# Attention and spectral mixing in one kernel: values in halves, a smaller reciprocal, moved splits, and half of the last transfers on GpSimd's queue

## The chip, the cores and the metric

The kernel runs on one core of a Trainium2 chip. The metric is the device time of one execution in microseconds, the median of several executions. TensorE is called PE here, VectorE DVE, ScalarE ACT, GpSimd POOL, and the engine that issues transfers SP.

## What is computed

The shapes are fixed: 8 batches, 12 heads, 448 tokens, heads of 64; 768 channels. First an attention with capped scores, then, on its output, a mixing over tokens and over channels, all in float32 (the weights arrive in float64):

```python
scores = np.matmul(q, k.transpose(0, 1, 3, 2)) / np.sqrt(64)
scores = cap * np.tanh(scores / cap)
attn = np.exp(scores - scores.max(-1, keepdims=True))
x = np.matmul(attn / (attn.sum(-1, keepdims=True) + 1e-09), v)   # then heads side by side: (8, 448, 768)
theta = x @ w_theta
y = w_tok_r @ (x * cos(theta)) + w_tok_i @ (x * sin(theta))       # over tokens, per batch
u = x + y
out = u + np.maximum(u @ w_ch, 0.0)
```

## The kernel before

Work goes pair by pair: a pair is two heads of one batch, so a batch has 6 pairs (NP) and the kernel 48 (NS). A step s of the outer loop computes the scores of pair s and finishes pair k = s-1. What a step does, and in which order, is written as a line of words (FRONT for steps 0 to 7, PARTS for a batch's six later steps, OTHER for single steps). The words are issued in that order, each engine runs its own instructions strictly in that order, and nothing is moved by a scheduler.

- `A`, `B` (line 216): scores of the pair's first and second half of the keys, on PE into one PSUM tile `s` of four banks, of which there is one. So B can start only when the tanh of A has read it, and the next A only when the tanh of B has.
- `tA`, `tB` (221) are the tanh, `eA`, `eB` (227) the exponentials, on ACT, into the tiles `p`.
- `V` (259): values times `p`, 16 matmuls for pair k, on PE; `cV` (265) copies the result to `x` on ACT.
- `R` (278): sums over keys by matmuls with ones, for two pairs at a time into one tile `r`; `R0`, `R1` are its two halves in FRONT. `I` (301): DVE takes 1/r of the whole 128x448 tile, in which each sum stands in 32 equal rows, and SP spreads it (305) into `bc`. `n`, `N` (309): DVE multiplies `x` by `bc`.
- `w0`, `w1`, `w2`: pieces of the weights' preparation, placed by the table WEIGHTS under (step, a/b/c). A float64 weight tile (`th0` to `th5` of w_theta, `ch0` to `ch5` of w_ch, `tk0` to `tk6` of the token weights) is loaded by SP (">", 106), scaled on ACT ("*", 110) or DVE ("#", 113), and split into a high and a low part on DVE (118 to 127). For `ch` tiles the cast of the high part (123) is on ACT, between DVE's instructions.
- `x`, `X`, `u`: split of an activation tile into high (ACT, 319) and low part (DVE, 320).
- `T` (328 to 330): theta of one channel block, 54 matmuls for three; `y` (350, 351), `d` (356 to 358), `sc` (363, 364), `r` (368): angle reduction, cosine and sine, product. `f` (372) turns 32x32 blocks on DVE, and `D` (381) carries the 32-row stripes to their places: 16 transfers from SP for one of the three pairs of blocks, D0, D1, D2. After them `h` and `l` (386, 392) split the turned blocks on ACT and DVE, `M` (401 to 403) mixes over tokens on PE, `m` (406) adds on DVE, `C` (328 to 330 with w_ch) and `c` (413) end a batch.

Steps 0 to 7 have scores, values and weights only; step 8 starts the first batch's theta. In the last batch no scores are left: its theta, C3 to C5 of the batch before and the three carries are one line of words (`OTHER[(B - 2, 5)]`), and its mixing another.

## Time and profile before

| what | value |
|---|---|
| median of 3 executions | 944.97 us (944.39 to 946.01) |
| profiled execution, its own time | 941.22 us |
| its span, first to last instruction | 939.4 us |
| PE / DVE / ACT busy | 98% / 73% / 66% |
| DMA | 90.66 MB, nearly all on one queue |

The profiled execution is 3.75 us shorter than the median, and 1.8 us of its time lie outside of the span. PE is busy almost throughout, so what matters is where it is not; a busy share of PE says nothing of its pace, since matmuls are pipelined and their ends are modelled. Starts of instructions are the safer reading.

### The profile page before, as it was taken

How to read it: one execution, taken by the hardware profiler on the slowest of the kernel's cores; microseconds unless marked ns; L12 is line 12 of the kernel's file. 1: busy time of each engine (PE TensorE's matmuls, PEld its weight loads, DVE VectorE, ACT ScalarE, POOL GpSimd, SP SyncE). 2: the span in 40 equal slices, each digit the busy share in tenths (PEclk: the TensorE clock that was granted, in tenths of full speed). 3: DMA queues.
4: the chain of work that ended last, by engine and by line, in shares of the span. 5: the costliest groups of instructions: out<-in, count | busy, mean ns of one | idle time of the engine just before them, and what ended most of it. 6: DMA issues, size and time to landing. Idle time of an engine off the chain costs nothing.

```text
span 939.4 us, 12874 instructions
## 1 busy us (share of the span) xinstructions
PE 916.8 (98%) x4912; PEld 660.9 (70%) x4912; DVE 682.9 (73%) x914; ACT 617.6 (66%) x644; POOL 0.4 (0%) x6
## 2 busy tenths in 40 slices
PE   8999989999999999999999999999999999999997
PEld 4224657667776787777677776776877777789887
DVE  5898756997876679666887568775787568965741
ACT  7988696567954688656976479645895569753420
POOL 0000000000000000000000000000000000000000
PEclk9999999999999999999999999999999999999999
DMA  7664155422642235332452325422353333411521
GB/s 267 200 186 128 34 123 132 121 98 72 126 89 79 82 65 120 78 108 70 86 102 67 101 62 107 117 78 71 67 119 80 91 96 76 77 32 48 92 52 62
DMA packets 208774, 90.66 MB, mean 97 GB/s; under 512 B 182464, under 2 KB 194752, under 8 KB 208704
## 3 DMA queue, kind: packets, MB, share of 16 engines
q1 hardware_dynamic: 208704, 89.76, 38.3%
q8 instruction: 40, 0.66, 0.3%
q14 instruction: 30, 0.25, 0.1%
HBM read 45.68 MB, written 11.01 MB: 60 GB/s over the span
## 4 chain that ended last, share of the span: by engine, by line
PE 73%; ACT 15%; DVE 6%; SPq 3%; DMA 1%; issue 1%; DVEq 0%; ACTq 0%
PE a L259 10%; PE s L216 10%; PE mx L403 7%; PE mx L401 7%; PE mx L402 7%; PE ch L328 6%; PE ch L329 6%; PE ch L330 6%; ACT p L221 5%; PE th L328 4%; PE th L329 4%; PE th L330 4%; SPq L381 3%; ACT p L227 2%; PE r L278 2%; ACT L221 2%
## 5 line engine op out<-in xcount | busy, mean ns | idle before, releaser
L221 ACT ACTIVATE p<-s,qscale 112x1792 f32<-112x1792 f32 x96 | 168.5, 1755 | 124.2 <-PE s L216 122.6
L227 ACT ACTIVATE p<-p,cap_sb 112x1792 f32<-112x1792 f32 x96 | 170.2, 1785 | 0.4
L259 PE MATMUL a<-p,v 112*64 112x448 f32 x768 | 155.1, 546 | 3.7 <-ACT p L227 3.7
L259 PEld LDWEIGHTS a<-p,v 112*64 112x64 f32 x768 | 50.7, 136 | 91.0 <-issue 74.9
L328 PE MATMUL ch<-us,wch_h 128*128 128x448 f32 x288 | 107.1, 372 | 0.0
L328 PE MATMUL th<-xs,wth_h 128*128 128x448 f32 x288 | 107.0, 371 | 0.0
L329 PE MATMUL ch<-us,wch_h 128*128 128x448 f32 x288 | 105.5, 366 | 0.0
L329 PE MATMUL th<-xs,wth_h 128*128 128x448 f32 x288 | 105.5, 366 | 0.0
L330 PE MATMUL ch<-us,wch_l 128*128 128x448 f32 x288 | 105.4, 366 | 0.0
L330 PE MATMUL th<-xs,wth_l 128*128 128x448 f32 x288 | 105.3, 366 | 0.0
L252 DVE TENSOR_TENSOR ps<-ps,p 112x896 f32<-112x896 f32 x76 | 82.8, 1089 | 2.2
L301 DVE RECIPROCAL ri<-r 128x448 f32<-128x448 f32 x24 | 70.9, 2954 | 17.2 <-PE r L278 17.2
L403 PE MATMUL mx<-wtk_h,zl_False 128*128 128x448 f32 x192 | 71.4, 372 | 3.2 <-DVE zl_False L392 2.5
L401 PE MATMUL mx<-wtk_h,zh_False 128*128 128x448 f32 x192 | 72.0, 375 | 0.1
L402 PE MATMUL mx<-wtk_l,zh_False 128*128 128x448 f32 x192 | 70.2, 366 | 0.0
L368 DVE TENSOR_TENSOR g_sb<-g_sb,x 128x896 f32<-128x896 f32 x48 | 50.7, 1086 | 22.3 <-ACT g_sb L364 22.3
L413 DVE SCALAR_TENSOR_TENSOR x<-ch,x 128x448 f32<-128x448 f32 x48 | 29.8, 620 | 51.1 <-PE ch L330 51.1
L328 PEld LDWEIGHTS ch<-us,wch_h 128*128 128x128 f32 x288 | 54.2, 188 | 10.3 <-issue 5.3
L328 PEld LDWEIGHTS th<-xs,wth_h 128*128 128x128 f32 x288 | 54.1, 188 | 9.6 <-issue 5.2
L330 PEld LDWEIGHTS ch<-us,wch_l 128*128 128x128 f32 x288 | 54.2, 188 | 4.9 <-DVE wch_l L127 0.2
L330 PEld LDWEIGHTS th<-xs,wth_l 128*128 128x128 f32 x288 | 54.1, 188 | 4.7
L329 PEld LDWEIGHTS th<-xs,wth_h 128*128 128x128 f32 x288 | 54.1, 188 | 4.6 <-DVE xs L320 0.3
(79 smaller groups left out, 1550.8 us busy)
## 6 DMA issues: line engine op xcount, KB each, us to landing
g_sb<-g_sb SPq DMA_DIRECT2D x384, 56.0 KB, 2.0
qk_sb<-in_qk SPq DMA_DIRECT2D x35, 448.0 KB, 3.6
v<-in_v SPq DMA_DIRECT2D x48, 224.0 KB, 2.9
bc<-ri SPq DMA_DIRECT2D x96, 112.0 KB, 2.3
out_dram<-x SPq DMA_DIRECT2D x48, 224.0 KB, 2.0
qk<-in_qk SPq DMA_DIRECT2D x13, 448.0 KB, 3.5
g_sb<-in_wth SPq DMA_DIRECT2D x6, 768.0 KB, 5.7
g_sb<-in_wch SPq DMA_DIRECT2D x6, 768.0 KB, 4.8
```

Of the source, the lines that this page charges most:

```text
L216: nc.tensor.matmul(sp[:CP, i, hh, :S], kk[k][rows, 1, ks], qq[k][rows, 0, :], start=n == 0, stop=n == len(products) - 1)
L221: nc.scalar.activation(pt[k, half], spt.pop((k, half))[:CP, :, :, :S], AF.Tanh, scale=qscale[:CP])
L227: nc.scalar.activation(pp, pp, AF.Exp, scale=cap_sb[:CP])
L252: nc.vector.tensor_tensor(pst[k], pst[k], pt[k, 1][:, i], op=ALU.add)
L259: nc.tensor.matmul(acc[hh * D : (hh + 1) * D, :S], va[:, hh, c, :], pt[k, c // 2][:, c % 2, hh, :], start=c == 0, stop=c == NCH - 1)
L301: nc.vector.reciprocal(ri, r[:, :S])
L328: nc.tensor.matmul(acc[:, :S], wh[:, j, ms], t[:, 0, :], start=j == 0, stop=False)
L329: nc.tensor.matmul(acc[:, :S], wh[:, j, ms], t[:, 1, :], start=False, stop=False)
L330: nc.tensor.matmul(acc[:, :S], wl[:, j, ms], t[:, 0, :], start=False, stop=j == NJ - 1)
L401: nc.tensor.matmul(acc[:, :S], zh, wtk_h[:, c, :], start=c == 0, stop=False)
L402: nc.tensor.matmul(acc[:, :S], zh, wtk_l[:, c, :], start=False, stop=False)
L403: nc.tensor.matmul(acc[:, :S], zl, wtk_h[:, c, :], start=False, stop=c == NC2 - 1)
```

## The change

1. In FRONT the values are computed in two halves: `Va` (keys of A) stays between A and B, `Vb` (keys of B) goes behind B. The copy `cV` goes behind the tanh of B.
2. `I` no longer takes 448 reciprocals in a row: DVE turns the 32x32 blocks of `r` into `ri`, takes the reciprocal of 14 columns into a small tile `few`, and turns these, repeated, back into `ri`. This holds for all 24 places.
3. Splits are moved among the steps, `th3` and `ch0` are scaled on DVE, and the cast of `ch0`, `ch1` and `ch2` is on DVE. The split of the first activation blocks is spread over steps 5, 6 and 7.
4. In steps 8 and 9 the exponentials stand directly behind their tanh, ahead of theta.
5. In the last batch 8 of the 16 transfers of D1 and of D2 (odd d) are issued from GpSimd's queue, and the first `l` stand ahead of r5 on DVE.

```diff
-            steps["ch", m] = Split(room_g(...), w_ch[m], wch_h[:, :, ms], wch_l[:, :, ms], True)
+            steps["ch", m] = Split(room_g(...), w_ch[m], wch_h[:, :, ms], wch_l[:, :, ms], m > 2)
...
-        (3, "c"): "*tk2", (4, "a"): "*th4", (4, "b"): "th4 >ch0", (4, "c"): "*tk3", (5, "b"): "tk2 >tk4 tk3 >tk5",
+        (4, "a"): "*th4 *tk2", (4, "b"): "th4 >ch0", (4, "c"): "*tk3", (5, "b"): "tk2 >tk4 tk3 >tk5",
...
+    def av(k, halves):
+        if 0 in halves:
+            acc_of["a", k] = psM.tile([P, 512], F32, tag="m", name=f"a{k}")
+        va, acc = vt[k], acc_of["a", k]
+        for c in (c for c in range(NCH) if c // 2 in halves):
...
         ri = wk.tile([P, S], F32, tag="ps", name=f"ri{k}", bufs=2)
+        nc.vector.transpose(out=ri, in_=r[:, :S])
+        few = wk.tile([P, S // 32], F32, tag="few", name=f"few{k}", bufs=1)
+        each = ri.rearrange("p (c j) -> p c j", j=32)[:, :, 0]
...
-            nc.vector.reciprocal(ri, r[:, :S])
+            nc.vector.reciprocal(few, each)
+        nc.vector.transpose(out=ri, in_=few.unsqueeze(2).broadcast_to([P, S // 32, 32]))
...
-                nc.sync.dma_start(t[32 * m : 32 * m + 32, :, d, :], z[32 * d : 32 * d + 32, :, m, :])
+                queue = nc.gpsimd if b == B - 1 and i and d % 2 else nc.sync
+                queue.dma_start(t[32 * m : 32 * m + 32, :, d, :], z[32 * d : 32 * d + 32, :, m, :])
...
-    FRONT = "A tA w0 eA V cV v R0 B tB R1 q w1 n I eB aA aB w2 x"
+    FRONT = "A tA w0 eA Va R0 B tB Vb cV v R1 q w1 n I eB aA aB w2 x"
...
-        (0, 0): "A tA V cV w0 v R I B tB q P w1 eA T0 y0 d0 aA eB T1 y1 d1 sc0 T2 y2 r0 r1 f0 f1 d2 w2 D0",
+        (0, 0): "A tA eA V cV w0 v R I B tB eB aA aB q T0 y0 d0 w1 T1 y1 d1 sc0 w2 T2 y2 r0 r1 f0 f1 d2 D0",
...
-                for j in {6: range(4), 7: range(4, NJ)}.get(s, ()):
+                for j in {5: range(2), 6: range(2, 4), 7: range(4, NJ)}.get(s, ()):
```

PE in step 3 and at the start of step 4 (a step without sums); `s_0` and `s_1` are the scores of A and B, `a` the values of the pair before, `p_0` and `p_1` its two halves. Before:

```order
L216 MATMUL s_0_292<-qk_206 112x448 x4
L259 MATMUL a_301<-p_0_227,v_197 64x448 x4
L259 MATMUL a_301<-p_1_258,v_197 64x448 x4
L216 MATMUL s_1_314<-qk_206 112x448 x4
L216 MATMUL s_0_342<-qk_272 112x448 x4
```

and with the change:

```order
L216 MATMUL s_0_295<-qk_206 112x448 x4
L260 MATMUL a_303<-p_0_227,v_204 64x448 x4
L216 MATMUL s_1_308<-qk_206 112x448 x4
L260 MATMUL a_303<-p_1_250,v_204 64x448 x4
L216 MATMUL s_0_344<-qk_272 112x448 x4
```

The second half of the values has moved from ahead of B to between B and the next A.

ACT at the end of step 11 and the start of step 12, around the split of `ch2`: line 110 scales it, line 123 casts its high part, the tanh that follows is A's of step 12. Before:

```order
L227 ACTIVATE p_1_1097<-p_1_1097,cap_sb 112x1792
L319 CAST us_2_1187<-x_310 128x448
L110 ACTIVATE g_sb<-g_sb 128x768
L123 CAST wch_h<-g_sb 128x6x128
L221 ACTIVATE p_0_1218<-s_0_1217,qscale 112x1792
```

and with the change:

```order
L227 ACTIVATE p_1_1112<-p_1_1112,cap_sb 112x1792
L325 CAST us_2_1202<-x_319 128x448
L110 ACTIVATE g_sb<-g_sb 128x768
L221 ACTIVATE p_0_1233<-s_0_1232,qscale 112x1792
L267 COPY x_1248<-a_1239 128x448
```

The cast is gone from ACT's row (it is on DVE); that of `ch4`, ahead of the tanh of step 13, stays.

DVE at the last batch's third pair of blocks: the first product (r4), the second (r5), the two block turns (f4, f5), the low parts `zl_0` for the first mixing, and the last additions of the batch before. Before:

```order
L368 TENSOR_TENSOR g_sb<-g_sb,x_6606 128x896
L368 TENSOR_TENSOR g_sb<-g_sb,x_6733 128x896
L372 STREAM_TRANSPOSE g_sb<-g_sb 128x896 x2
L413 SCALAR_TENSOR_TENSOR x_5686<-ch_4_7066,x_5686 128x448
L392 TENSOR_TENSOR zl_0_False<-g_sb,zh_0_False 128x512
L392 TENSOR_TENSOR zl_0_True<-g_sb,zh_0_True 128x384
```

and with the change:

```order
L374 TENSOR_TENSOR g_sb<-g_sb,x_6675 128x896
L399 TENSOR_TENSOR zl_0_False<-g_sb,zh_0_False 128x512
L399 TENSOR_TENSOR zl_0_True<-g_sb,zh_0_True 128x384
L374 TENSOR_TENSOR g_sb<-g_sb,x_6802 128x896
L378 STREAM_TRANSPOSE g_sb<-g_sb 128x896 x2
L420 SCALAR_TENSOR_TENSOR x_5746<-ch_4_7146,x_5746 128x448
```

The low parts of the first mixing now stand ahead of r5 and of both turns.

## Rows read from the trace of the kernel before

**Rows 1.** Page part 1: busy time, share of the span, instructions of each engine.

```profile
PE 916.8 (98%) x4912; PEld 660.9 (70%) x4912; DVE 682.9 (73%) x914; ACT 617.6 (66%) x644; POOL 0.4 (0%) x6
```

**Rows 2.** Waits: engine, line <- releaser: total us, times, longest us.

```profile
PE s L216 <- ACT p L221: 8.7, 9, 1.9
```

**Rows 3.** Timeline of PE, steps 4 to 8: start, us, engine, line [idle before <-releaser].

```profile
40.05 1.76 PE L216 MATMUL s<-qk 64*112 64x448 f32 x8 [1.93 <-ACT p L221]
41.74 3.23 PE L259 MATMUL a<-p,v 112*64 112x448 f32 x16
44.90 1.71 PE L278 MATMUL r<-p,ones_sb 112*32 112x448 f32 x16
46.54 1.76 PE L216 MATMUL s<-qk 64*112 64x448 f32 x8
...
55.00 1.76 PE L216 MATMUL s<-qk 64*112 64x448 f32 x8
58.62 1.76 PE L216 MATMUL s<-qk 64*112 64x448 f32 x8 [1.85 <-ACT p L221]
...
79.12 1.76 PE L216 MATMUL s<-qk 64*112 64x448 f32 x8 [0.54 <-ACT p L221]
```

**Rows 4.** Timeline of ACT: the last activation split ahead of step 8's tanh.

```profile
82.94 1.10 ACT L319 CAST xs<-x 128x448 fp32r<-128x448 f32 x2 [0.94 <-DVE x L309]
```

**Rows 5.** Timeline of PE in step 10.

```profile
125.36 1.72 PE L259 MATMUL a<-p,v 112*64 112x448 f32 x8 [2.72 <-ACT p L227]
128.08 1.72 PE L259 MATMUL a<-p,v 112*64 112x448 f32 x8 [1.00 <-ACT p L227]
129.74 3.20 PE L278 MATMUL r<-p,ones_sb 112*32 112x448 f32 x16
```

**Rows 6.** Groups by line: count | busy us, mean ns | idle before, releaser.

```profile
L301 DVE RECIPROCAL ri<-r 128x448 f32<-128x448 f32 x24 | 70.9, 2954 | 17.2 <-PE r L278 17.2
L372 DVE STREAM_TRANSPOSE g_sb<-g_sb 128x896 f32<-128x896 f32 x48 | 51.1, 1092 | 0.0
L125 DVE CAST wth_h<-g_sb 128x768 fp32r<-128x768 f32 x6 | 3.4, 562 | 0.0
```

**Rows 7.** Timelines of ACT and PE, steps 12 and 13.

```profile
172.12 0.84 ACT L123 CAST wch_h<-g_sb 128x768 fp32r<-128x768 f32 x1 [4.64 <-DVE g_sb L119]
191.02 0.84 ACT L123 CAST wch_h<-g_sb 128x768 fp32r<-128x768 f32 x1 [4.08 <-DVE g_sb L119]
...
174.66 3.00 PE L216 MATMUL s<-qk 64*112 64x448 f32 x8 [1.66 <-ACT p L221]
194.02 1.76 PE L216 MATMUL s<-qk 64*112 64x448 f32 x8
```

**Rows 8.** Stretch, then busy us by engine, PE's granted clock, DMA share, GB/s.

```profile
175.00:178.40 3.40, 3.40 (x10) 1.41 (x7) 3.40 (x5) 2.06 (x5) 0.00 (x0) 0.50 0.48 128
```

**Rows 9.** Timelines of the last batch: SP, PE, ACT, DVE.

```profile
866.33 21.92 SPq L381 DMA_DIRECT2D g_sb<-g_sb  x32
...
885.05 0.47 PE L403 MATMUL mx<-wtk_h,zl_False 128*128 128x448 f32 x1 [1.45 <-DVE zl_False L392]
903.83 0.47 PE L403 MATMUL mx<-wtk_h,zl_False 128*128 128x448 f32 x1 [1.05 <-DVE zl_False L392]
...
901.43 0.62 ACT L386 CAST zh_False<-g_sb 128x512 fp32r<-128x512 f32 x1 [5.11 <-DMA g_sb<-g_sb]
...
872.98 2.10 DVE L372 STREAM_TRANSPOSE g_sb<-g_sb 128x896 f32<-128x896 f32 x2
877.01 0.39 DVE L357 TENSOR_SCALAR g_sb<-g_sb 128x448 f32<-128x448 f32 x1
881.79 2.10 DVE L372 STREAM_TRANSPOSE g_sb<-g_sb 128x896 f32<-128x896 f32 x2
884.32 0.67 DVE L392 TENSOR_TENSOR zl_False<-g_sb,zh_False 128x512 fp32r<-128x512 f32 x1
```

**Rows 10.** Page part 6: DMA issues: count, KB each, median us to landing.

```profile
g_sb<-g_sb SPq DMA_DIRECT2D x384, 56.0 KB, 2.0
```

More of the change, by code (lines that the diff above doesn't have):

```diff
@@ L148, in weight_steps @@
             steps["th", m] = Split(room_g((0, 6 * S)[m % 2]), w_theta[m], wth_h[:, :, ms], wth_l[:, :, ms])
-            steps["ch", m] = Split(room_g((0, 6 * S, 8 * S, 0, 8 * S, 0)[m]), w_ch[m], wch_h[:, :, ms], wch_l[:, :, ms], True)
+            steps["ch", m] = Split(room_g((0, 6 * S, 8 * S, 0, 8 * S, 0)[m]), w_ch[m], wch_h[:, :, ms], wch_l[:, :, ms], m > 2)
         for c in range(NC2):
@@ L252, in add_half @@
                 nc.vector.tensor_tensor(pst[k], pst[k], pt[k, 1][:, i], op=ALU.add)
-    def av(k):
-        va = vt.pop(k)
-        acc = psM.tile([P, 512], F32, tag="m", name=f"a{k}")
-        for c in range(NCH):
+    def av(k, halves):
[3 more added lines that the diff above has]
+        for c in (c for c in range(NCH) if c // 2 in halves):
             for hh in range(2):
@@ L260, in av @@
                                  start=c == 0, stop=c == NCH - 1)
-        acc_of["a", k] = acc
+        if 1 in halves:
+            vt.pop(k)
     def av_out(k):
@@ L296, in invert @@
         ri = wk.tile([P, S], F32, tag="ps", name=f"ri{k}", bufs=2)
+        nc.vector.transpose(out=ri, in_=r[:, :S])
+        few = wk.tile([P, S // 32], F32, tag="few", name=f"few{k}", bufs=1)
+        each = ri.rearrange("p (c j) -> p c j", j=32)[:, :, 0]
         if state["general"]:
-            nc.vector.tensor_scalar_add(ri, r[:, :S], 1e-9)
-            nc.vector.reciprocal(ri, ri)
-        else:
-            nc.vector.reciprocal(ri, r[:, :S])
+            nc.vector.tensor_scalar_add(few, each, 1e-9)
+            nc.vector.reciprocal(few, few)
+        else:
+            nc.vector.reciprocal(few, each)
+        nc.vector.transpose(out=ri, in_=few.unsqueeze(2).broadcast_to([P, S // 32, 32]))
         for n in (k - 1, k):
@@ L427, in softcap_attn_then_spectral_mix @@
     OTHER = {
-        (0, 0): "A tA V cV w0 v R I B tB q P w1 eA T0 y0 d0 aA eB T1 y1 d1 sc0 T2 y2 r0 r1 f0 f1 d2 w2 D0",
-        (0, 1): "A tA V cV N w0 v R I aB- B tB q P w1 T3 y3 d3 sc1 eA T4 r2 r3 f2 f3 D1 y4 d4 eB T5 aA aB y5 d5 w2",
+        (0, 0): "A tA eA V cV w0 v R I B tB eB aA aB q T0 y0 d0 w1 T1 y1 d1 sc0 w2 T2 y2 r0 r1 f0 f1 d2 D0",
+        (0, 1): "A tA eA V cV N v R I B tB eB aA aB q T3 y3 d3 sc1 T4 r2 r3 f2 f3 D1 y4 d4 T5 y5 d5",
         (B - 2, 4): "V cV u3 u4 u5 R I C0 c0 C1 X0 X1 c1 C2 X2 X3 c2",
         (B - 2, 5): "N X4 X5 T0+ y0+ d0+ T1+ y1+ d1+ sc0+ T2+ r0+ r1+ f0+ f1+ D0+ y2+ d2+ T3+ y3+ d3+ sc1+ T4+ r2+ r3+ f2+ f3+ D1+ y4+ d4+"
-                    " T5+ y5+ d5+ sc2+ C3 c3 r4+ r5+ f4+ f5+ D2+ C4 c4 h0a+ l0a+ h0b+ l0b+ h1a+ C5 c5",
+                    " T5+ y5+ d5+ sc2+ C3 c3 r4+ h0a+ l0a+ h0b+ l0b+ r5+ f4+ f5+ D2+ C4 c4 h1a+ C5 c5",
         (B - 1, 0): "M0a l1a h1b M0b l1b h2a m0 u0 M1a l2a h2b M1b l2b h3a m1 u1 M2a l3a h3b M2b l3b h4a m2 u2 M3a l4a h4b M3b l4b h5a"
@@ L465, in run @@
                     add_half(s, "AB".index(word[1]))
-            elif word == "V":
+            elif name == "V":
                 if done:
-                    av(k)
+                    av(k, (0, 1) if word == "V" else ("ab".index(word[1]),))
             elif word == "cV":
```

6 rows, old and new, of the table WEIGHTS are left out of this document.

## The prediction, made before the changed kernel ran

> **What bounds the kernel now.** I read the busy shares first, then the waits, then the timelines around the largest. PE is busy for 916.8 of 939.4 us [rows 1], so at most 22.6 us can come from filling its idle time; the rest would need fewer matmuls, and the change has as many as before. The waits say where the idle time is: 8.7 us before scores that wait for a tanh [rows 2], 3.72 us before values that wait for an exponential (2.72 and 1.00, step 10) [rows 5], and 2.5 us in the last batch before matmuls that wait for low parts (1.45 and 1.05) [rows 9]. DVE, at 73%, is full only where weights are split, and POOL does nothing. The sum is made from starts of instructions, against the profiled execution: 941.22 us of its own time, a span of 939.4 and 1.8 around it. It lies 3.75 us under the median of 944.97, so I carry the gain over to the median.
>
> **Part 1, values in halves (steps 1 to 8).** Of the two-half `s` there is one set, so the next scores wait for the tanh of the last ones. In a step without sums the second scores start at 55.00 and the next step's at 58.62 with 1.85 of idle before them [rows 3]: 3.62 us for scores, semaphore and tanh, under which only 1.69 us of matmuls lie (40.05 to 41.74), since the values (3.16, to 44.90) all stand on the other side, ahead of B. With halves, each tanh is covered by half the values: 1.66 (128.08 to 129.74) [rows 5], so A + Va is 1.69 + 1.66 = 3.35, still under 3.62, and such a step takes 2 x 3.62 = 7.24. A step with sums has also half of the sums (1.64, 44.90 to 46.54) on each side: 2 x (1.69 + 1.66 + 1.64) = 9.98, more than the tanh. The two steps make 17.22; before, from 40.05 to 58.62, they made 18.57 [rows 3]. That is 1.35 for steps 4 and 5, and again for 2 and 3, which have waits of the same sizes. Steps 6 and 7 both have sums: 58.62 to 79.12 is 20.50, and becomes 19.96, so 0.5. With 0.2 in step 1 part 1 gives 3.4, if ACT is free at each tanh.
>
> Where it may not be is step 8. The tanh of A stands there behind the last activation splits on ACT, which wait for DVE's products until 82.94 [rows 4], and DVE is packed ahead of those. The change gives DVE back three reciprocals' difference by then and adds the scales of `th3` and `ch0` and a cast: three passes over 128x768 at 0.56 each [rows 6], 1.7 in all. The new `I` is two block turns of 448 columns and a reciprocal of 14. A turn of 896 columns is 1.09 [rows 6]; by columns one of 448 is 0.55, with a fixed part between that and 1.09. The short reciprocal lies between 0.1 (2.954 x 14/448) and some 0.2. So `I` costs 1.2 to 2.4 us against 2.954; I take 1.4, since DVE's other instructions go nearly by columns. Then the splits start at 82.94 - 3 x 1.55 + 1.7 = 80.0, the tanh at 81.1 and B could start at 82.9, while PE comes there at 83.5 (75.5 for A, then 1.69 + 3.16 and 3.2 of sums). It just fits, by 0.6.
>
> **Part 2, steps 8 to 10.** With the exponentials directly behind their tanh, values of the next step no longer find them outstanding. The 2.72 and 1.00 [rows 5] go, and the two restarts cost some 0.15 each beside them: 4.0. What is late next is the angle work of theta on ACT, now queued behind both exponentials; the 54 matmuls of three blocks lie over it on PE. The bounds are 4.0 and, where the wait only moves to those angles, 0.
>
> **Part 3, step 12.** The tanh of A stands behind the cast of `ch2` on ACT, which waits 4.64 us for DVE and runs at 172.12; PE waits 1.66 for it, until 174.66 [rows 7]. From 175.0 to 178.4 the granted clock is 0.50, the lower level of 1.2 GHz [rows 8], right after that idle time, and eight matmuls take 3.00 where they take 1.76 elsewhere. Half of 3.4 us is 1.7. With the cast on DVE (0.56 there, hidden) both go: 1.66 + 1.7 = 3.4. But the cast of `ch4` stays on ACT ahead of the tanh of step 13. It waits 4.08 for DVE and runs at 191.02, and PE started B there at 194.02 without idle time [rows 7]. DVE's row up to it is shortened by about 1.1 us (one reciprocal, less a cast), so B can start at about 192.5 to 192.9, while PE, 3.4 earlier, is there at 190.6. So 1.9 is waited again, and 1.5 is left. A step back to the lower clock after this wait, as after 174.66, would take most of the rest.
>
> **Part 4, the other eighteen `I`.** DVE gets 24 x 1.55 = 37 us back in all. After step 13 no wait of PE among those named above ends on it, so I count 0; of what else PE is idle, 22.6 - 8.7 - 3.7 - 2.5 = 7.7 us at most, mostly around loads at the start, a little could go, 0.6.
>
> **Part 5, the tail.** The low parts of the first mixing stand behind r5 and two turns on DVE (881.79 to 883.89, then 884.32) [rows 9]; ahead of r5 they are done long before PE asks at 883.6. The 1.45 goes. For that the last turns end 1.2 us later (0.67 [rows 9] and by columns 0.5), and D2 can be issued from 885.1 instead of 883.9. Before, that did not matter: 32 transfers of D0 and D1 took 21.92 us on SP, 0.685 each [rows 9], so D2 began only at about 889 and its end held ACT until 901.43 and PE until 903.83, 1.05 idle [rows 9]. With two queues SP has 8 of D1 (877.3 to 882.8) and 8 of D2 (885.1 to 890.6). GpSimd's queue can begin its 8 of D1 when the turns end at 875.1 (872.98 + 2.10), and its D2 at 885.1 or when D1 is issued. PE, without waits, needs D2 some 1.5 to 2.5 us earlier than it came: by about 899.2; D1 by about 890.9. With p us for a transfer on GpSimd's queue the last one is out at 875.1 + 16p or 885.1 + 8p; with 2.0 to landing [rows 10], p up to 1.4 is in time.
>
> No transfer on GpSimd's queue is in this trace. The nearest rows are SP's: 0.685 if it issues as SP does, and 2.0 [rows 10] if each waits until the one ahead has landed. I take a value within the first half of this, since nothing in the rows makes one transfer wait for the one before. Then both waits go, with 0.3 more for each restart: 3.1. With p = 2.0, landing included by what that bound means, the last has landed at 875.1 + 32 = 907.1, 7.9 late.
>
> A rule bears on this. In the stretch from 875.1 DVE has four instructions at the fast pace of 0.39 us for 448 columns (as at 877.01), 1.6 us in all [rows 9]. The Trainium skill (SBUF - State Buffer, section "Who interferes with whom", and the box ahead of "A bandwidth-pool intuition that's wrong") says that descriptors of a GpSimd transfer are written by GpSimd, which is shut out while DVE runs in a mode that takes two ports; it gives 620 ns alone against about 3100 ns beside such an operation. By that rule, if only those four instructions block, Pool is at most 1.6 us later and the sum stays. If every transfer took 3.1, the sixteenth would be out at 924.7, 25.5 late, and the time would be about 958. No row here shows either.
>
> **Sum.** 3.4 + 4.0 + 1.5 + 0 + 3.1 = 12.0 us: a span of about 927.4, a profiled time of 929.2, and on the median 944.97 - 12.0 = 933.0.
>
> **The rivals.**
> (a) GpSimd's queue is slow, and the last carry takes the place of the wait removed. For it: POOL issues nothing now, so its pace is unknown, and the slack is only 2.0 - 1.4 = 0.6 us a transfer. Against it: there are only 16, on one stretch of 24 us. At p = 2.0 the time is 933.0 + 7.9 = 940.9; every further 0.1 costs 1.6. From p = 2.4 on it is above 946.9 and ends on the other side, slower than before: at p = 3.0 the last is 24 us late and the time 957.
> (b) DVE is late at step 8, and less comes from the front. With `I` at 2.35 in place of 1.4 the three cost 2.85 more, B of step 8 is ready 2.2 late, and the time is 935.2. For it: the margin is 0.6 us. Against it: turns of 896 columns run at nearly DVE's pace by columns.
> (c) The halves shorten nothing, because two groups of 8 matmuls alternate with scores and each restart costs, or because ACT is not free: 3.4 are lost, and the change does not do what it says in front: 936.4. With the lower clock after step 13's wait it would be 938.
> (d) More is gained: step 13 does not wait (1.9), some of the 7.7 goes (0.6): 930.5.
>
> **How the numbers follow.** Two tenths of a percent, 1.9 us, is about what a measurement of this kernel can tell from no change. Forecast, within 2 us of 933.0 (931 to 935): 0.46. (b) and (c), 935 to 939: 0.18. (a) with p of 1.5 to 2.3, 937 to 945: 0.15; with p of 2.3 to 2.4, 945 to 947: 0.03. (a) with p above 2.4, slower: 0.10. (d), under 931: 0.08. The range goes from 929.5, which is (d) with a scatter of 1 us, to 942, which is (a) with p of 2.07; left out above are the slower case, the 0.03 and some 0.06 of (a) above 942, and a little of (d) below. Faster is 0.46 + 0.18 + 0.15 + 0.08 = 0.87, same 0.03, slower 0.10.
>
> **What would show it.** Right: in step 4 scores start 4.99 us apart and in step 5 3.62 apart; A of step 8 is at about 75.5; no idle before values in step 10, and the first mixing about 7.4 earlier; no stretch at the lower clock at 170, and 1.9 of idle before B of step 13; both waits in the last batch gone, with GpSimd's sixteenth transfer out before 897 on the clock of before. Wrong: an `I` of more than 1.6 us in its three instructions and a wait at step 8; transfers on GpSimd's queue more than 1.4 us apart, and ACT's high parts in the last batch waiting for their landing, which alone could turn the gain into a loss.

## The result, and the profile after the change

The changed kernel ran at 929.74 us (median of 5, 927.67 to 931.85) beside 944.97 for the kernel before: a ratio of 0.9835 (95% interval 0.982 to 0.985), or 15.2 us less by the medians and 15.6 by the ratio. The forecast was 933.0, 12.0 less, with a range of 929.5 to 942.0. The median lies at its very edge, and by the ratio (0.9835 x 944.97 = 929.4) it is just below: the gain was larger than the range allowed. The profiled execution took 927.67 us, its span is 925.9, so profile against profile the gain is 13.5.

Page part 1 of the changed kernel (busy time, share, instructions): PE is 4.4 us less busy with the same 4912 matmuls ([rows 1]). Some 1.7 of that is the lower clock that Part 3 counts; the rest is the first sign of something that was not in the sum.

```profile
PE 912.4 (99%) x4912; PEld 661.1 (71%) x4912; DVE 653.0 (71%) x967; ACT 613.8 (66%) x639; POOL 10.8 (1%) x22
```

Starts of the same instructions in both traces tell in which stretch the time was won (us from the first instruction; the last column is the forecast for the stretch):

| point on PE | before | after | won so far | in this stretch | forecast |
|---|---|---|---|---|---|
| A of step 8 | 79.12 | 75.79 | 3.33 | 3.3 | 3.4 |
| first mixing, step 10 | 134.56 | 127.22 | 7.34 | 4.0 | 4.0 |
| B of step 13 | 194.02 | 184.79 | 9.23 | 1.9 | 1.5 |
| last batch's first mixing | 883.02 | 870.95 | 12.07 | 2.8 | 0 |
| its first channel matmul | 912.09 | 898.28 | 13.81 | 1.7 | 3.1 |
| end of the span | 939.4 | 925.9 | 13.5 | -0.3 | 0 |

The two mixings and the first channel matmul of the table, before and after (the other points are in [rows 3], [rows 7] and below):

```profile
134.56 0.47 PE L401 MATMUL mx<-wtk_h,zh_False 128*128 128x448 f32 x1
883.02 0.37 PE L401 MATMUL mx<-wtk_h,zh_False 128*128 128x448 f32 x1
912.09 0.36 PE L328 MATMUL ch<-us,wch_h 128*128 128x448 f32 x1
```

```profile
127.22 0.48 PE L408 MATMUL mx<-wtk_h,zh_False 128*128 128x448 f32 x1
870.95 0.36 PE L408 MATMUL mx<-wtk_h,zh_False 128*128 128x448 f32 x1
898.28 0.36 PE L334 MATMUL ch<-us,wch_h 128*128 128x448 f32 x1
```

Three stretches came as forecast, one gave 2.8 us that nobody had counted, and the tail gave half. First the three. PE in steps 4, 5 and 8 (start, us, engine, line, count [idle before <- releaser]):

```profile
38.68 1.76 PE L216 MATMUL s<-qk 64*112 64x448 f32 x8 [0.20 <-ACT p L221]
40.37 1.72 PE L260 MATMUL a<-p,v 112*64 112x448 f32 x8
42.02 1.71 PE L280 MATMUL r<-p,ones_sb 112*32 112x448 f32 x16
43.66 1.76 PE L216 MATMUL s<-qk 64*112 64x448 f32 x8
...
52.26 1.76 PE L216 MATMUL s<-qk 64*112 64x448 f32 x8 [0.20 <-ACT p L221]
...
55.88 1.76 PE L216 MATMUL s<-qk 64*112 64x448 f32 x8 [0.20 <-ACT p L221]
...
75.79 1.76 PE L216 MATMUL s<-qk 64*112 64x448 f32 x8
...
83.77 1.76 PE L216 MATMUL s<-qk 64*112 64x448 f32 x8
```

Where [rows 3] have waits of 1.9, 0.2 is left. Scores start 4.98 apart in the step with sums (38.68 to 43.66) and 3.62 in the one without (52.26 to 55.88). B of step 8 starts at 83.77 without idle time: the activation splits ahead of it ran in time on ACT, at 79.96 where [rows 4] have 82.94:

```profile
79.96 1.10 ACT L325 CAST xs<-x 128x448 fp32r<-128x448 f32 x2 [3.46 <-DVE x L315]
```

The new `I`, as groups by line (count | busy us, mean ns | idle before). Two turns and the short reciprocal are 1.53 us, 1.61 with the gaps between them, against 2.95 in [rows 6]; the forecast took 1.4:

```profile
L307 DVE STREAM_TRANSPOSE ri<-few 128x448 f32<-128x448 f32 x24 | 15.5, 645 | 0.8
L299 DVE STREAM_TRANSPOSE ri<-r 128x448 f32<-128x448 f32 x24 | 15.5, 645 | 14.5 <-PE r L280 14.5
L306 DVE RECIPROCAL few<-ri 128x14 f32<-128x14 f32 x24 | 5.8, 243 | 0.8
```

PE in steps 10, 12 and 13. The values of step 10 no longer wait ([rows 5]: 2.72 and 1.00), step 12's B no longer waits, and step 13's B waits 1.58 where 1.9 was forecast:

```profile
119.25 3.23 PE L260 MATMUL a<-p,v 112*64 112x448 f32 x16
...
165.25 1.76 PE L216 MATMUL s<-qk 64*112 64x448 f32 x8
...
184.79 1.76 PE L216 MATMUL s<-qk 64*112 64x448 f32 x8 [1.58 <-ACT p L221]
```

The granted clock at that place (stretch, busy us of PE, PEld, DVE, ACT and POOL, granted clock, DMA share, GB/s) is 1.00 now, the level of 2.4 GHz, where [rows 8] have 0.50; after the 1.58 it stayed there too:

```profile
166.00:170.00 4.00, 4.00 (x20) 2.79 (x17) 3.93 (x7) 2.96 (x3) 0.00 (x0) 1.00 0.22 29
184.00:189.00 5.00, 4.21 (x20) 2.98 (x21) 4.86 (x7) 3.50 (x4) 0.00 (x0) 1.00 0.28 92
```

The tail. PE, ACT and POOL in the last batch:

```profile
890.08 0.47 PE L410 MATMUL mx<-wtk_h,zl_False 128*128 128x448 f32 x1 [1.30 <-DVE zl_False L399]
```

```profile
887.43 0.62 ACT L393 CAST zh_False<-g_sb 128x512 fp32r<-128x512 f32 x1 [4.99 <-DMA g_sb<-g_sb]
```

```profile
863.70 0.89 POOL L388 DMA_DIRECT2D g_sb<-g_sb  x1 [862.81 <-DVE g_sb L362]
...
867.50 1.30 POOL L388 DMA_DIRECT2D g_sb<-g_sb  x2 [1.93 <-DMA g_sb<-g_sb]
...
883.81 1.34 POOL L388 DMA_DIRECT2D g_sb<-g_sb  x2 [0.96 <-issue]
```

The 1.45 at the first mixing of [rows 9] is gone, but the second wait stands: 1.30 where it was 1.05. GpSimd's queue issues its 16 transfers from 863.70 to 885.15, 1.34 us each on average, twice SP's 0.67, and SP has issued its own share of D2 at 878.28 (872.96 + 5.32). So the last carry now ends on GpSimd's queue, not on SP's; its last transfer has landed at 886.74.

### The profile page after: what moved, and what is told of

It is laid out like the page before. It is cut to its first block, busy times and chain, and to the rows that moved or that the text cites. A ratio compares the mean times of both kernels' runs of the same rounds, so it can differ in the third digit from the quotient of the medians.

```text
span 925.9 us, 12930 instructions
## 1 busy us (share of the span) xinstructions
PE 912.4 (99%) x4912; PEld 661.1 (71%) x4912; DVE 653.0 (71%) x967; ACT 613.8 (66%) x639; POOL 10.8 (1%) x22
## 4 chain that ended last, share of the span: by engine, by line
PE 80%; ACT 11%; DVE 5%; issue 1%; DMA 1%; SPq 1%; DVEq 0%; ACTq 0%
PE s L216 11%; PE a L260 11%; PE mx L410 7%; PE mx L408 7%; PE mx L409 7%; PE ch L334 6%; PE ch L336 6%; PE ch L335 6%; PE th L334 5%; PE th L335 5%; PE th L336 5%; ACT p L221 4%; PE r L280 4%; ACT L221 2%; ACT p L227 1%
## 5 line engine op out<-in xcount | busy, mean ns | idle before, releaser
L362 DVE SCALAR_TENSOR_TENSOR g_sb<-g_sb 128x448 f32<-128x448 f32 x48 | 29.5, 615 | 46.7 <-ACT g_sb L357 46.7
L334 PEld LDWEIGHTS ch<-us,wch_h 128*128 128x128 f32 x288 | 54.1, 188 | 9.6 <-issue 4.6
L335 PEld LDWEIGHTS ch<-us,wch_h 128*128 128x128 f32 x288 | 54.2, 188 | 4.6 <-DVE us L326 0.3
```

Of the source, the lines that this page charges most:

```text
L334: nc.tensor.matmul(acc[:, :S], wh[:, j, ms], t[:, 0, :], start=j == 0, stop=False)
L335: nc.tensor.matmul(acc[:, :S], wh[:, j, ms], t[:, 1, :], start=False, stop=False)
```

## Experiments

Ratios are to executions of the kernel before that were taken beside each run; the changed kernel's is 0.9835. One thousandth is 0.95 us. A difference "by the medians" is between two times, one "by the ratios" between two such ratios. Each experiment starts from the changed kernel unless it says otherwise.

### The 2.8 us of the batches

From the first mixing of one batch to that of another four batches later, before and after (timelines of PE, one fence for each kernel):

```profile
360.16 0.47 PE L401 MATMUL mx<-wtk_h,zh_False 128*128 128x448 f32 x1
...
802.20 0.47 PE L401 MATMUL mx<-wtk_h,zh_False 128*128 128x448 f32 x1
```

```profile
350.44 0.48 PE L408 MATMUL mx<-wtk_h,zh_False 128*128 128x448 f32 x1
...
790.61 0.47 PE L408 MATMUL mx<-wtk_h,zh_False 128*128 128x448 f32 x1
```

A batch took 442.04 / 4 = 110.51 us and takes 110.04. PE has no wait in these batches above 0.11, in either kernel. Start by start, the mixing's matmuls went 204 ns apart before and go 200 to 202.3 now; theta's and the channels' go at 204 in both. What differs for the mixing alone is a place: the new tile `few` (56 bytes a partition, 64 with padding) is allocated ahead of `zh`, so `zh` lies 64 bytes further. Theory A is this place, rival B the work moved around the mixing.

**e1_shift_only**: the kernel before, with such a tile and no other change.

```diff
+        if k == 1:
+            few = wk.tile([P, S // 32], F32, tag="few", name=f"few{k}", bufs=1)
+            nc.gpsimd.memset(few, 0.0)
```

> The kernel before with one unused tile of 56 bytes a partition (64 with its padding) ahead of the tiles bc and zh, written once on GpSimd; nothing else is changed. In the changed kernel the mixing of steps 14 to 47 goes at some 200 to 202 ns from one matmul to the next, where it took 204, and a batch takes 110.04 us in place of 110.50; zh lies 64 bytes further there, because the tile of the 14 reciprocals stands ahead of it. Theory A (place): this kernel alone shows the faster mixing, a batch of 110.0 to 110.1 and 2.5 to 3.5 us less in all. Rival B (the smaller reciprocal or the moved work lets the mixing run faster): a batch stays at 110.5 and the time is that of the kernel before within 1 us.

```profile
360.85 0.47 PE L404 MATMUL mx<-wtk_h,zh_False 128*128 128x448 f32 x1
...
801.19 0.47 PE L404 MATMUL mx<-wtk_h,zh_False 128*128 128x448 f32 x1
```

A batch takes 110.09, as theory A has it. The ratio is 0.9981 (0.9964 to 0.9999), 1.8 us, and 2.7 by the medians, where theory A had 2.5 to 3.5; the mixing goes at 200 to 202.3 in all but one of its stretches (204.4). A tile that nothing reads makes the kernel before faster.

**e2_no_tile**: `few` put into the unused half of the tile that `ri` lies in, so `zh` is back at its old place.

```diff
-        ri = wk.tile([P, S], F32, tag="ps", name=f"ri{k}", bufs=2)
+        both = wk.tile([P, 2, S], F32, tag="ps", name=f"ri{k}", bufs=2)
+        ri = both[:, 0, :]
...
-        few = wk.tile([P, S // 32], F32, tag="few", name=f"few{k}", bufs=1)
+        few = both[:, 1, : S // 32]
```

> The changed kernel with its 14 reciprocals in the unused half of the tile that ri lies in, so that zh is back at its old place; the instructions and their order are the same. Theory A (place): the mixing is back at 204 ns a matmul, a batch at 110.5, and the time 2.5 to 3.5 us above the changed kernel. Rival B: a batch stays at 110.04 and the time is the same.

```profile
352.90 0.47 PE L409 MATMUL mx<-wtk_h,zh_False 128*128 128x448 f32 x1
...
794.84 0.47 PE L409 MATMUL mx<-wtk_h,zh_False 128*128 128x448 f32 x1
```

A batch takes 110.49 again, the mixing 204 ns a matmul, and the time is 932.31 (0.9855, 0.9833 to 0.9878): 2.6 above the changed kernel by the medians and 1.9 by the ratios, whose intervals overlap. The traces are clearer than the times. From B of step 13 to the last batch's first mixing it takes 689.00 us in the kernel before, 686.16 in the changed kernel, and 688.89 here. Same instructions, same order: theory A holds from both sides, and B falls. How much the tile is worth varies: in the other kernels below whose tiles lie as in the changed kernel, this stretch takes 686.1 to 687.8 (e8_long_reciprocal left out, which has a lower clock in it), 1.1 to 2.8 less than here.

**e3_pad_wk**: e2_no_tile, with 64 bytes ahead of all work tiles.

```diff
     g_sb = const.tile([P, 16 * S], F32, name="g_sb")
+    pad = const.tile([P, 16], F32, name="pad")
```

> As e2_no_tile, with a pad of 64 bytes behind g_sb, so that all work tiles lie 64 bytes further: zh as in the changed kernel, zl, xs, us, v, p, hi and lo 64 further than there, the weights where they were. If the pace of a matmul hangs on where its two operands lie towards each other, the matmuls of theta and of the channels (204 ns in both kernels) go at 200 to 202 too: 216 a batch by 2 to 4 ns make 3.5 to 7 us less than the changed kernel. If it is something of zh alone, the time is that of the changed kernel within 1 us.

```profile
350.96 0.48 PE L412 MATMUL mx<-wtk_h,zh_False 128*128 128x448 f32 x1
...
789.31 0.47 PE L412 MATMUL mx<-wtk_h,zh_False 128*128 128x448 f32 x1
```

A batch takes 109.59. Mixing goes at 200.0, theta and channels at 202.2, and the time is 925.46, 0.9776 (0.9752 to 0.980): 4.3 us less than the changed kernel by the medians, and 6.9 less than e2_no_tile, from which it differs by the pad alone (and one instruction on GpSimd that fills it). Its interval overlaps neither of theirs.

**e15_pad_all, e10_pad_32B, e11_pad_96B** (one execution each): the pad ahead of the weights, so that all lies as far from each other as in e2_no_tile; and the pad of e3_pad_wk with 32 and with 96 bytes.

```diff
+    pad = const.tile([P, 16], F32, name="pad")
     wth_h = const.tile([P, NJ, DM], F32R, name="wth_h")
```

> As e2_no_tile, with the 64-byte pad ahead of the weights, so that weights, activations, zh and zl all lie 64 bytes further and as far from each other as in e2_no_tile. If the pace of a matmul hangs on where its two operands lie towards each other, all of theta, mixing and channels go at 204 ns again, as in e2_no_tile. If it hangs on where zh, xs and us lie by themselves, they go at 200 to 202 as in e3_pad_wk.

> As e3_pad_wk with a pad of 32 bytes in place of 64: 0 bytes gave 204 ns for theta, mixing and channels, 64 gave 202.2, 200.0 and 202.2. If any shift against the weights does it, as fast as with 64; if it must be 64, 204.

> As e3_pad_wk with a pad of 96 bytes: by a period of 128 bytes it stands to 64 as 32 does, and goes as e10_pad_32B goes.

**e16_three_apart**: e14_pad_and_four (below), with three small constants allocated behind the weights of theta and channels, so that these lie 96 bytes nearer the start.

```diff
     cap_sb = const.tile([P, 1], F32, name="cap_sb")
...
+    wth_h = const.tile([P, NJ, DM], F32R, name="wth_h")
...
     qscale = const.tile([P, 1], F32, name="qscale")
```

> e14_pad_and_four with three small constants allocated behind the weights of theta and of the channels instead of ahead of them: these weights lie 96 bytes nearer the start, so that xs and us stand 32 bytes (by a period of 128) off the weights, as in e10_pad_32B, while zh and zl stay 64 off theirs; nothing else moves. Theory (the distance of the two operands by a period of 128 bytes sets the pace, for each pair of tiles by itself): theta and channels at 200.1 to 200.4 ns a matmul in place of 202.2, mixing at 200.0, so 216 x 8 x 2 ns = 3.4 us less than e14_pad_and_four's 924.72: 921.3, a ratio of 0.9738. Rival: more than the distance counts, and theta stays at 202 or the mixing goes back to 204 or above: 924 or more.

Nanoseconds from one matmul to the next, and the distance of the two operands' tiles from each other, in bytes, whole multiples of 128 left out:

| kernel | xs, us to weights | theta, channels | zh / zl to weights | mixing |
|---|---|---|---|---|
| before, e2_no_tile | 0 | 204.0 | 0 / 0 | 204.0 |
| e15_pad_all (all 64 further) | 0 | 204.0 | 0 / 0 | 204.0 |
| after, e1_shift_only | 0 | 204.0 | 64 / 0 | 200.0 or 202.3, seldom 204.4 |
| e3_pad_wk, e14_pad_and_four | 64 | 202.2 | 64 / 64 | 200.0 |
| e10_pad_32B | 32 | 200.1 to 200.4 | 32 / 32 | 205.3 |
| e11_pad_96B | 96 | 204.4 | 96 / 96 | 206.5 or 200.0 |
| e16_three_apart | 32 | 200.0 and 206.4 | 64 / 64 | 200.0 |

The three took 935.04 (e15_pad_all), 928.56 (e10_pad_32B) and 931.96 us (e11_pad_96B). e15_pad_all is the one that tells: with everything 64 bytes further the pace is 204.0 again, so it is the place of one operand towards the other, not of one alone. But the distance by a period of 128 is not the whole rule. At one and the same distance the changed kernel's mixing goes at 200.0 in some batches and at 202.3 in others, and e9_ch2_cast_act and e12_ch1_as_before (below), whose tiles lie as in the changed kernel, have 204.4 in 4 of 13 stretches. In e16_three_apart theta runs at 200.0 in one step of a batch and at 206.4 in the next, and its time is 925.05 (0.978), no better than e14_pad_and_four's: its rival held. What the rule is stays open.

### The tail

**e4_four_on_pool**: 4 in place of 8 of the 16 transfers on GpSimd's queue.

```diff
-                queue = nc.gpsimd if b == B - 1 and i and d % 2 else nc.sync
+                queue = nc.gpsimd if b == B - 1 and i and d == 1 else nc.sync
```

> The changed kernel with 4 in place of 8 of the 16 transfers of D1 and of D2 on GpSimd's queue. In the changed kernel these are 1.3 to 1.4 us apart and the last has landed 13.9 us after the turns of r4 and r5, at 886.7, while SP has issued its own at 878.3; PE waits 1.30 us at 890.08. Theory: SP needs 12 x 0.67 = 8.0 us and GpSimd's queue 4 x 1.35 = 5.4 us, so the last has landed some 10.5 us after the turns, 883.5, and the wait of 1.30 falls to 0: 1.3 to 1.6 us less than the changed kernel. Rival: the wait of PE is set by the low parts' chain on DVE and ACT and not by the landing: the same time.

```profile
875.33 1.27 POOL L388 DMA_DIRECT2D g_sb<-g_sb  x2 [4.85 <-DVE x L420]
877.90 0.64 POOL L388 DMA_DIRECT2D g_sb<-g_sb  x1 [1.30 <-issue]
879.08 0.63 POOL L388 DMA_DIRECT2D g_sb<-g_sb  x1 [0.53 <-POOLq L536]
```

GpSimd's share is out 7.1 us after the first mixing (872.60) instead of 14.2 (885.15 - 870.95), and no wait above 0.15 is left in the last batch. The time is 927.73, 0.9803 (0.978 to 0.9826): 2.0 less by the medians, 3.0 by the ratios. In the trace the tail, from the last batch's first mixing to its first channel matmul, takes 25.22 in place of 27.33: 2.1, more than the wait of 1.30, since the restarts and a small wait ahead of it go too (0.5) and this mixing goes at 200.1 ns in place of 202.2 (0.3). So the wait hung on the landing, and half of the transfers was too many for a queue with twice SP's price.

The wait can cost more than the changed kernel's own trace shows. With four transfers the tail takes 25.2 in all four kernels that have them (e4_four_on_pool, e5_all, e14_pad_and_four, e16_three_apart). With eight it takes 26.9 to 28.1 in nine traces, but 29.1 in e6_whole_values, 29.0 in e9_ch2_cast_act and 30.5 in e15_pad_all. In these three the same wait is followed by 3.4 us at a granted clock of 0.50, as here in e6_whole_values (PE, then the stretch after it):

```profile
895.73 0.64 PE L410 MATMUL mx<-wtk_h,zl_False 128*128 128x448 f32 x1 [1.31 <-DVE zl_False L399]
```

```profile
895.90:899.30 3.40, 3.40 (x10) 3.01 (x11) 1.40 (x3) 0.57 (x1) 0.00 (x0) 0.50 0.00 0
```

**e14_pad_and_four** (pad and four transfers) and **e5_all** (these and the cast of ch4 on DVE):

```diff
-            steps["ch", m] = Split(room_g(...), w_ch[m], wch_h[:, :, ms], wch_l[:, :, ms], m > 2)
+            steps["ch", m] = Split(room_g(...), w_ch[m], wch_h[:, :, ms], wch_l[:, :, ms], m in (3, 5))
```

> The pad of e3_pad_wk and the 4 transfers of e4_four_on_pool, with the cast of ch4 left on ACT: in e5_all its move to DVE took the wait of step 13 away and made one of 1.85 us at 196.25, before the matmuls that use ch4's low part, with 3.4 us at a granted clock of 0.50 behind it. Theory: 1.3 to 1.6 us less than e3_pad_wk's 925.46, that is 923.9 to 924.2, a ratio of 0.976. Rival: the scatter of the clock hides it.

> The changed kernel with three things more: the 64-byte pad of e3_pad_wk, 4 of 16 transfers on GpSimd's queue as in e4_four_on_pool, and the cast of ch4 on DVE instead of ACT (those of ch3 and ch5 stay). e3_pad_wk ran at 925.46, e4_four_on_pool 2.0 under the changed kernel. Theory: the waits of 1.30 in the last batch and of 1.58 before B of step 13 go, 1.3 to 1.6 and some 1.6 less than e3_pad_wk: 922.0 to 922.8, a ratio to the kernel before of 0.974 to 0.976. Rival: the cast on DVE, 0.56 longer in a full row, makes ch4's split late for its matmuls, and step 13 gains nothing: 924.

They ran at 924.72 (0.9774) and 924.65 (0.9770), each less than the changed kernel and equal to each other. Against e3_pad_wk (0.9776) neither shows a gain in the ratio, so the rival of each held. The tail is shorter all the same (25.2 in both, 26.92 in e3_pad_wk); the times do not show it clear of their scatter. In e5_all the wait of step 13 is gone and another has come, since DVE is now later with ch4's low part, with the lower clock behind it (timeline of PE, then the stretch after it):

```profile
196.25 0.47 PE L340 MATMUL ch<-us,wch_l 128*128 128x448 f32 x1 [1.85 <-DVE wch_l L128]
```

```profile
197.60:200.90 3.30, 3.30 (x10) 2.95 (x9) 3.27 (x6) 1.84 (x4) 0.00 (x0) 0.50 0.37 139
```

### The front and steps 8 to 13, part by part

**e6_whole_values**: part 1 undone alone.

```diff
-    FRONT = "A tA w0 eA Va R0 B tB Vb cV v R1 q w1 n I eB aA aB w2 x"
+    FRONT = "A tA w0 eA V cV v R0 B tB R1 q w1 n I eB aA aB w2 x"
```

> The changed kernel with the values of steps 1 to 7 in one piece ahead of B, as before (part 1 undone alone). In the changed kernel A of step 8 starts at 75.79, 70.4 us after the first instruction of PE that waits for its scale (5.37); before, 74.1 after it. Theory: the waits of 1.9 before scores come back, A of step 8 is 3.4 to 3.7 later and the time as much longer. Rival: the cheaper reciprocal and the moved splits alone have freed ACT, and less than half of that comes back.

```profile
10.86 1.39 PE L216 MATMUL s<-qk_sb 64*112 64x448 f32 x6 [0.18 <-ACT p L221]
...
41.71 1.76 PE L216 MATMUL s<-qk 64*112 64x448 f32 x8 [1.85 <-ACT p L221]
...
80.48 1.76 PE L216 MATMUL s<-qk 64*112 64x448 f32 x8 [0.23 <-ACT p L221]
```

The waits are back. From the second half of step 0's scores to A of step 8 it takes 69.62 (80.48 - 10.86), in the changed kernel 66.31 (75.79 - 9.48): 3.3 us. The time is 934.62 (0.9866), 2.9 more by the ratios and 4.9 by the medians. Part 1 is worth what was forecast.

**e8_long_reciprocal**: one reciprocal over 448 columns again; `few` is kept, so that the places stay.

```diff
-        nc.vector.transpose(out=ri, in_=r[:, :S])
...
-            nc.vector.reciprocal(few, each)
-        nc.vector.transpose(out=ri, in_=few.unsqueeze(2).broadcast_to([P, S // 32, 32]))
+            nc.vector.reciprocal(ri, r[:, :S])
```

> The changed kernel with one reciprocal over 448 columns again; the small tile is kept and written once, so that all tiles lie where they lie in the changed kernel. I took 1.61 us there (0.65, 0.24 and 0.65 with gaps) against 2.95. Theory: three of them ahead of step 8 delay the last activation splits from 79.96 by 4.0 to 84.0, B of step 8 starts 3.1 late, and in step 13 one delays the cast of ch4 by 1.35: 3.1 + 1.3 = 4.4 us longer. Rival: DVE's row has room, nothing waits, and the time is the same within 1 us: then the smaller reciprocal is not part of the gain.

```profile
87.82 0.63 PE L216 MATMUL s<-qk 64*112 64x448 f32 x2 [2.07 <-ACT p L221]
...
191.76 1.09 PE L216 MATMUL s<-qk 64*112 64x448 f32 x2 [2.87 <-ACT p L221]
```

```profile
88.40:91.70 3.30, 3.30 (x11) 1.48 (x8) 3.23 (x5) 3.11 (x4) 0.00 (x0) 0.50 0.02 5
190.80:197.50 6.70, 5.74 (x15) 3.30 (x16) 5.04 (x7) 3.63 (x4) 0.00 (x0) 0.50 0.24 74
```

935.64, 0.9880: 4.3 us by the ratios, 5.9 by the medians. Both waits come where they were expected, at step 8 (2.07) and at step 13 (2.87, 1.3 more), and the trace has the lower clock around both. A batch takes 110.03, as in the changed kernel: the smaller reciprocal saves nothing in the batches, where nothing waits for DVE, and 4 to 6 us in two steps.

**e7_late_exps**: part 2's order undone alone. **e12_ch1_as_before**: the exponentials early, but ch1 split in step 9 with its cast on ACT. **e13_ch1_and_exps**: both.

```diff
-        (0, 0): "A tA eA V cV w0 v R I B tB eB aA aB q T0 y0 d0 w1 T1 y1 d1 sc0 w2 ...",
-        (0, 1): "A tA eA V cV N v R I B tB eB aA aB q T3 y3 d3 sc1 T4 r2 r3 f2 f3 D1 y4 d4 T5 y5 d5",
+        (0, 0): "A tA V cV w0 v R I B tB q eA T0 y0 d0 w1 aA eB T1 y1 d1 aB sc0 w2 ...",
+        (0, 1): "A tA V cV N v R I B tB q T3 y3 d3 sc1 eA T4 r2 r3 f2 f3 D1 y4 d4 eB T5 aA aB y5 d5",
```

```diff
-            steps["ch", m] = Split(room_g(...), w_ch[m], wch_h[:, :, ms], wch_l[:, :, ms], m > 2)
+            steps["ch", m] = Split(room_g(...), w_ch[m], wch_h[:, :, ms], wch_l[:, :, ms], m > 2 or m == 1)
...
-        (8, "b"): "tk6 *ch1", (8, "c"): "ch1",
+        (8, "b"): "tk6 *ch1", (9, "a"): "ch1",
```

> The changed kernel with the exponentials of steps 8 and 9 behind theta's first work again (part 2 undone alone). Theory: waits of about 2.7 and 1.0 before the values of step 10 come back, 4.0 us longer. Rival: with the cheaper splits of the front ACT comes to them earlier, and under 2 come back.

> e7_late_exps lost nothing against the changed kernel (929.38 and 929.74, no wait in step 10), so the order of the exponentials is not what removed the 3.72 us. In the kernel before ACT waits 5.86 us in step 9 for DVE at the cast of ch1 (114.11), ahead of the tanh of B. Here the changed kernel has the split of ch1 back in step 9 with its cast on ACT; the exponentials stay early. Theory: it is this cast that makes the exponentials late; with them early a part comes back, 1 to 3 us of waits in steps 9 and 10. Rival: with the exponentials early the cast costs nothing, so either of the two moves is enough.

> As e12_ch1_as_before, and the exponentials late as in e7_late_exps. Theory (the cast is the cause): waits of about 2.7 and 1.0 before the values of step 10 are back, 3 to 4 us longer than e7_late_exps. Rival: the cheaper reciprocal and the other moved splits have given DVE and ACT enough room, and under 1.5 us come back.

e7_late_exps ran at 929.38 (0.9812) and e12_ch1_as_before at 930.73 (0.9844), neither with a wait in step 10: the theory of each fell and its rival held. Only both together bring waits back, and 1.43 of the 3.72, not the 3 to 4 expected (931.84, 0.9853); PE in step 10 of e13_ch1_and_exps:

```profile
121.11 1.72 PE L260 MATMUL a<-p,v 112*64 112x448 f32 x8 [0.43 <-ACT p L227]
123.84 0.60 PE L260 MATMUL a<-p,v 112*64 112x448 f32 x2 [1.00 <-ACT p L227]
```

By starts, from A of step 8 to the first mixing it takes 55.43 before, 51.43 with the change, 51.46 in e7_late_exps, 51.43 in e12_ch1_as_before and 53.15 in e13_ch1_and_exps.

Where the time goes shows on ACT in step 9, before and then in e13_ch1_and_exps:

```profile
114.11 0.84 ACT L123 CAST wch_h<-g_sb 128x768 fp32r<-128x768 f32 x1 [5.86 <-DVE g_sb L119]
```

```profile
109.85 0.84 ACT L123 CAST wch_h<-g_sb 128x768 fp32r<-128x768 f32 x1 [3.54 <-DVE g_sb L119]
```

In the kernel before ACT waits 5.86 us for DVE to come to ch1, with the cast of ch1's high part at its head and the tanh of B behind that. In e13_ch1_and_exps it waits 3.54. What is left changed there is DVE's row: in the kernel before, the split of the token weight `tk6` lies directly ahead (107.78 to 111.53), and the change has moved it to an earlier place. So three edits shorten the same wait: the order of the exponentials, the move of ch1, and the move of a split out of DVE's row. Which of them gave the 4.0 us has no answer. Either of the first two is enough on top of the third; that the third gave the 2.3 that do not come back here is read from DVE's row, since no run undoes it together with the other two.

**e9_ch2_cast_act**: part 3's cast of ch2 back on ACT.

```diff
-            steps["ch", m] = Split(room_g(...), w_ch[m], wch_h[:, :, ms], wch_l[:, :, ms], m > 2)
+            steps["ch", m] = Split(room_g(...), w_ch[m], wch_h[:, :, ms], wch_l[:, :, ms], m > 1)
```

> The changed kernel with the cast of ch2 on ACT again (part 3 undone alone). Theory: the tanh of A of step 12 stands behind it, B waits some 1.7 to 1.9, but then the wait of 1.58 before B of step 13 is gone, because that B is held by the cast of ch4 at a time that hangs on DVE; alone it costs 0.3, and 2.0 if the granted clock falls to 0.50 for 3.4 us after the wait, as in the kernel before. Rival: both waits add up, 1.7 to 1.9 at full clock and 3.5 with the lower.

```profile
168.99 1.01 PE L216 MATMUL s<-qk 64*112 64x448 f32 x4 [1.74 <-ACT p L221]
...
186.74 1.76 PE L216 MATMUL s<-qk 64*112 64x448 f32 x8
```

931.15, 0.9836: no loss. The wait of step 12 is back at full clock, and that of step 13 is gone. From step 1's B, which starts at 19.77 here and at 17.86 in the changed kernel, B of step 13 comes 166.97 and 166.93 later: ch4's cast sets it, whatever happens in step 12.

## Why the prediction fell short

Profile against profile the gain is 13.5 where the sum had 12.0. The difference of 1.5 is made of four: 2.8 that Part 4 put at nothing, 0.3 more in Parts 1 to 3, 1.4 less in Part 5, and 0.3 lost behind it, which no run explains. That the four largely cancel is luck. Another 1.7 lie between the gain of the profiles and that of the medians.

**Parts 1 to 3, the sizes right.** Forecast 8.9 us up to B of step 13, measured 9.2, and 0.35 of that is the faster mixing of the first batch (the two halves of it ahead of that B took 13.05 us each and take 12.95 and 12.80). The step spacings of 4.99 and 3.62, the start of step 8 (75.5 against 75.79), the splits at 80.0 (79.96) and the new wait in step 13 (1.9 against 1.58) came as worked out. The method was to take each engine's row, find what ends last, and carry it to the next thing that is late.

**Parts 2 and 3, the owners wrong.** I gave the 4.0 to the order of the exponentials and the 3.4 of step 12 to the cast of ch2. Undoing either alone loses nothing that could be measured. The wait in step 10 named an exponential, and I moved the exponential; I did not look for what had held ACT ahead of it. For step 12 the net of 1.5 was near because I carried the chain on to ch4's cast, and in part by luck. The sum took 1.7 for the lower clock behind the wait of step 12 [rows 8]. e1_shift_only, which has the same order, waits as long there and keeps its clock; eight scores take 1.76, not 3.00:

```profile
176.66 1.76 PE L216 MATMUL s<-qk 64*112 64x448 f32 x8 [1.69 <-ACT p L221]
```

From the first mixing to B of step 13 it takes 58.30 us there, 59.47 in the kernel before and 57.57 in the changed one. So where the clock does not fall Part 3 gives some 0.7, not 1.5.

**Part 4, put at 0, is the step that failed:** 2.8 us. I asked only what DVE's saved time was worth there, and that it is worth nothing was right (e8_long_reciprocal). The pace of a matmul was taken as given: the first paragraph lets a gain come from PE's idle time or from fewer matmuls alone. And the new small tile was taken as having no price; it moved `zh` by 64 bytes, and that is worth 2.7 us of this stretch (688.89 in e2_no_tile against 686.16; 1.1 to 2.8 in other kernels with the same places). Nothing in the trace of before could show it. A comparison of where the tiles lie before and after would have shown that `zh` moves, though not what that is worth.

**Part 5, put at 3.1, is the term that was mis-sized:** 1.7, of which some 0.2 is the mixing's pace (126 matmuls at 202.2 ns where they took 204). The first wait went, as worked out; the second did not. The price of GpSimd's queue lay at the upper end of what I took, 1.34 us a transfer, and under the limit of 1.4. The limit was wrong. I let D2 land at 899.2 on the clock of before. On the changed kernel's clock, 12.07 earlier, that is 887.1; PE was ready at 888.78 (890.08 - 1.30), and from ACT's start on the landed blocks (887.43) to PE's start it takes 2.65: the high part, a cast of `us` and DVE's subtraction for it stand in between. ACT starts 0.7 after the last landing (886.74), so for PE at 888.78 that landing was needed at 888.78 - 2.65 - 0.7 = 885.4, or 897.5 on the clock of before. My own sum could have told: before, the last transfer of D2 landed at 901.05, and with 3.1 us taken out of PE's row ahead of its use it is needed 3.1 earlier, at about 898, not 1.5 to 2.5.

GpSimd's first transfer was its slowest: it starts at 863.70 and has landed at 867.19, 3.5 us later, while DVE runs its four fast instructions (863.53 to 865.76), and a gap of 1.93 ends at 867.50. The median from issue to landing is 2.2, and two others take 3.2 and 3.3 with none of these beside them. The Trainium skill (SBUF - State Buffer, section "A bandwidth-pool intuition that's wrong") gives about 620 ns for a transfer alone and about 3100 beside a copy on DVE that blocks it. Here every transfer is slower than the first of these figures and 13 of 16 are faster than the second; no run separates a block by DVE from other causes. The case of the prediction in which every transfer blocks fell: the sixteenth was out at 885.15, or 897.2 on the clock of before, not at 924.7.

**Median against profile.** The gain was carried from profiled executions to medians, and there it is 1.7 larger (15.2 against 13.5). The sum was made on an execution of 941.22 us, which is below all 45 times of the kernel before that were taken beside the experiments (941.24 to 950.65). One reason shows in the traces. In the profiled executions of both kernels the first eight scores take 1.76 us and B of step 0 starts at 9.14 (before) and 9.48 (after); in the traces of all sixteen experiments it starts at 10.65 to 12.00, and in e9_ch2_cast_act, for one, the first eight scores take 3.33. But both profiled executions have this early start, so it explains why each lies under its median and not the difference. Nor does the mean granted clock: it is 0.994 over the 45 executions of the kernel before and 0.998 over the 5 of the changed kernel, and the two profiled ones differ by as much (0.996 and 1.000). Where the 1.7 come from is open.

**The rivals.** (a) was the right place and came to a wait of 1.3, not a loss. Its range was not worked out as stated: by its own 1.6 us for each 0.1 below 940.9 at p = 2.0, p = 1.5 gives 932.9 and not 937. (b) did not come: a block turn took 0.645 us where columns alone gave 0.55, but the margin of 0.6 at step 8 held, and e8_long_reciprocal shows what it was worth. (c) fell. (d), more gain, is what happened, by a mechanism that I had not named.

## What to carry to other kernels

A wait's releaser is the last link, which need not be the cause: before an edit is credited, ask what held the releaser, and expect several edits to shorten one wait, so that each undone alone costs nothing. A transfer moved to a slower queue should be split by the price of each queue, and its deadline counted back through every instruction between landing and use, on every engine. A new small tile can move others: compare where the operands of the hot matmuls lie before and after, since a few nanoseconds on thousands of matmuls are microseconds.

## What the runs showed of the hardware

- The pace of float32r matmuls of 128x128 by 448 columns ran from 200.0 to 206.5 ns with nothing changed but the place of tiles in SBUF: 204.0 where the operands' tiles lie a multiple of 128 bytes apart (the kernel before, e2_no_tile, e15_pad_all), mostly 200.0 to 202.3 where they lie 64 apart, with 204.4 in a few stretches. The exact rule is open.
- GpSimd's queue takes 1.34 us from one transfer of 56 KB in 32 partitions to the next where SP takes 0.67. With four transfers in a row it took 1.1 (the last four of e4_four_on_pool).
- A short wait of PE is followed by a stretch at a granted clock of 0.50 in some executions and not in others. After 1.31 us in the last batch it was 0.50 for 3.4 us in e6_whole_values, e9_ch2_cast_act and e15_pad_all, and 1.00 in the changed kernel, e3_pad_wk and e12_ch1_as_before. After the wait of step 12 it was 0.50 for 3.4 us in the kernel before (1.66) and 1.00 in e1_shift_only (1.69). Around the wait of 2.87 in e8_long_reciprocal it was 0.50 for 6.7 us.
- DVE's reciprocal of 14 columns takes 0.24 us, of 448 columns 2.95; a block turn of 448 columns 0.645.
